# Forgetting attention and a bilinear FFN on one core: q and k turned on VectorE, scores of four heads on row quarters

## The chip, the cores and the metric

The kernel runs on one core of a Trainium2 chip. The core has a matrix engine (TensorE, "PE" in the profile, whose weight loads are listed apart as "PEld"), VectorE ("DVE"), ScalarE ("ACT") and GpSimd ("POOL"), each with its own in-order queue of instructions, and a queue "SP" that issues transfers. All work from SBUF, 128 partitions wide; TensorE writes to PSUM, which has eight banks of 512 float32 columns per partition. The metric is the device time in microseconds.

## The reference

Batch 8, 8 heads, 576 positions, 64 elements per head; FFN with model width 512 and inner width 1536, over 8 x 576 = 4608 tokens.

```python
scores = 0.125 * q @ k.T                      # per batch and head, 576 x 576
cum    = cumsum(log(clip(f, 1e-4, 1)))        # per batch and head
scores = where(causal, -1e9, scores + cum[i] - cum[j])
attn   = softmax(scores, -1);  o = attn @ v
x      = o, heads side by side: (4608, 512)
out    = ((x @ w_a) * (x @ w_b)) @ w_out      # (4608, 512)
```

In the softmax cum[i] is constant along a row and drops out, so the kernel only subtracts cum[j].

## The kernel before, in words

Work is cut into operations (`Op`). A list of numbers written out by hand, `ORDER` (line 1016), gives the sequence in which all operations are issued; each engine takes its own in that order. `CHOICE` (line 1123) is a string of letters that says which engine does an operation that several could do. What waits for what is worked out from the tiles that the operations touch.

There are 32 head pairs t = 0 to 31, four to a batch. A pair here is head pr and head pr + 4 of batch b = t // 4.

- **Inputs** (`batch_inputs`, line 310). q and k come in halves, four loads a batch, nine tokens of each of two heads on a partition; GpSimd casts them to 16 bits (in batch 0 ScalarE and VectorE help). `pe_transpose` (279) turns a half on TensorE: 18 transposes of 64 columns into two PSUM tiles of the ring "ff". `pe_evict` (290) copies each to qT or kT on ScalarE or VectorE, so that a head's 64 elements lie on partitions 0 to 63 or 64 to 127.
- **Scores** (`qk_group`, 411). The causal rows are cut into row blocks i = 0 to 4 (four of 128 queries, one of 64), in stages (1, 0), (2), (3), (4). Two heads are computed at once, on the two row halves of the array. The last block of 64 queries of both heads uses the whole array, with the queries laid out block-diagonally in `qd` by GpSimd (`last_queries`, 474). The score tiles "sc" hold two PSUM banks each, and there are two of them.
- **Decay and mask.** In batch 0 the decay row and the causal mask are added by further matmuls (`crow`, `pick`, `low`, `neg`); in batch 1 the decay row is spread to all partitions by a matmul (`spread_mm`, 480); from batch 2 on it is loaded from DRAM (`load_spread`, 491) and masked on GpSimd (`mask_copy`, `mask_last`).
- **Softmax.** VectorE adds the decay and takes the maximum in one instruction per head and block (`do_decay`, 516, line 540 in the profile; in batch 0 only a maximum, 514), ScalarE takes the exponential (571, 567), VectorE the reciprocal, GpSimd scales the probabilities (`do_norm`, 583, line 589).
- **Turning the probabilities.** In batch 0 on TensorE (`pe_tr`, 605) with evictions; from batch 1 by transposing transfers on SP's queue (`do_tr`, 599).
- **Values** (`do_pv`, 618, and `do_pv4`, 636 for the last 64 queries): for each key block and row block one matmul of 128 columns per head, the two heads on the two column halves. From batch 2 on, a pair's values are computed two pairs later, right after the score stage 0 of that later pair, and the last 64 queries' values go to a spare corner of that stage's score tile.
- **FFN** (`ffn`, 952). Token chunks of 256, 256, 256, 384, six of 512, and 384. Each needs all attention of its tokens. Twelve steps: `psa` and `psb` (four matmuls each, line 914), a copy of psa to SBUF (`ff_copy`), a product on VectorE (`ff_mul`, 925); then `pso` (934), an eviction and a store for each 128 tokens.

PSUM: two "sc" tiles of two banks, one "pv" bank, three "ff" banks. TensorE's order mixes FFN groups of earlier tokens between the attention stages of later ones.

Of the kernel before, what the change touches and what calls it, by code (L numbers as in the profile page):

```python
# [15 lines left out]
ADD = mybir.AluOpType.add  # L16
MIN = mybir.AluOpType.min
MAX = mybir.AluOpType.max

NEGBIG = -60000.0  # L20
SUB = mybir.AluOpType.subtract
AXX = mybir.AxisListType.X
# [3 lines left out]
def kernel(  # L26
# [17 lines left out]
    sbw = [min(128, S - 128 * i) for i in range(NSB)]  # L44
    BH = B * H
    NP = H // 2
    SF = 512
    ST = S - SF

    def pool(name, bufs=1, **kw):  # L50
        return ctx.enter_context(tc.tile_pool(name=name, bufs=bufs, **kw))

    perm = pool("perm")

    HP = [slice(0, 64), slice(64, 128)]
    dram = pool("scr", 1, space=bass.MemoryType.DRAM)

    neg64 = perm.tile([128, 64], FP16, tag="neg64", name="neg64")  # L60
    low = [perm.tile([128, 128], FP16, tag=f"low{i}", name=f"low{i}") for i in range(2)]

    qd = [perm.tile([128, 128], FP16, tag=f"qd{i}", name=f"qd{i}") for i in range(2)]
    lowd = perm.tile([128, 128], FP16, tag="lowd", name="lowd")

    crow = perm.tile([128, S], FP16, tag="crow", name="crow")
    pick = perm.tile([128, 32], FP16, tag="pick", name="pick")
    pickh = [perm.tile([128, 32], FP16, tag=f"pick{h}", name=f"pick{h}") for h in range(2)]
    ident16 = perm.tile([128, 128], FP16, tag="ident16", name="ident16")
    warm = perm.tile([128, 1], FP32, tag="warm", name="warm")  # L70

    def constants():
        make_identity(nc, ident16)
        for x in pickh:
            nc.gpsimd.memset(x, 0.0)
        for m in range(4):
            x = slice(32 * m, 32 * m + 32)
            nc.gpsimd.tensor_copy(out=pick[x, :], in_=ident16[x, x])
            nc.gpsimd.tensor_copy(out=pickh[m // 2][x, :], in_=ident16[x, x])
        nc.gpsimd.memset(neg64, 0.0)  # L80
        for x in low:
            nc.gpsimd.memset(x, 1.0)
        for h in range(2):
            nc.gpsimd.affine_select(out=neg64[HP[h], :], in_=neg64[HP[h], :],
                                    compare_op=mybir.AluOpType.not_equal, fill=NEGBIG, base=0,
# [6 lines left out]
    def paddings():  # L92
        for x in (*qd, lowd):
            nc.gpsimd.memset(x, 0.0)
        for r in HP:
            nc.gpsimd.tensor_copy(out=lowd[r, r], in_=low[0][r, 0:64])
# [104 lines left out]
    for o in o_f:  # L201
        o.issue, o.units = 0.5, 32
# [968 lines left out]
```

## Time and profile before

| | |
|---|---|
| median of 3 runs | 418.18 us (417.76 to 418.24) |
| span of the profiled execution | 416.2 us |
| busy: TensorE, VectorE, ScalarE, GpSimd | 386.7, 298.1, 283.4, 265.7 us |
| first FFN matmul | 35.58 us |
| scores, on TensorE (tile sc, last-query values in it) | 59.4 us busy |
| q/k transposes, on TensorE | 15.65 us busy |
| FFN, on TensorE (psa, psb, pso) | 115.25, 115.33, 98.78 us busy |

The profiled execution's span, 416.2 us, runs from its first to its last instruction; the runs' times also have some 2 us around it. A row of the groups of instructions reads: source line, engine, operation, output <- inputs, for matmuls the shape rows*columns of the array that is used, shapes, count, then busy time and mean duration of one in ns, then the idle time before the group and what ended it. A row of the timeline reads: start, duration, engine, line, operation, count. Matmuls overlap, so the time that one costs is the distance to the next start and not its duration.

### The profile page before, as it was taken

Reading aid. Unit: us, or ns where it says so; the run is one execution under the profiler, and the core shown is the slowest. Engines: PE = TensorE matmul, PEld = TensorE weight load, DVE = VectorE, ACT = ScalarE, POOL = GpSimd, SP = SyncE. Lnnn points to the kernel's source line nnn. Section 1 sums busy time; section 2 is a strip of 40 time slices with the busy share of each in tenths; the row PEclk is TensorE's granted clock in tenths of the full one; section 3 lists DMA queues with packets and bytes.
Section 4 is the critical chain, followed back from the end, with each engine's and each line's share of the span. In section 5 each row is a group of like instructions: output and inputs, shape, how many; then the busy total and the mean of one; then the engine's idle time right before and its main releaser. Section 6 shows DMA issues by size and latency. Waiting matters only on the chain.

```text
span 416.2 us, 10864 instructions
## 1 busy us (share of the span) xinstructions
PE 386.7 (93%) x3788; PEld 207.7 (50%) x3788; DVE 298.1 (72%) x1000; ACT 283.4 (68%) x797; POOL 265.7 (64%) x491
## 2 busy tenths in 40 slices
PE   2678999998989999999999999999999999999996
PEld 1346775756645544444454444454454444444552
DVE  3697998997878878786877888777877785332240
ACT  5788998986766877876777887677767783232231
POOL 5998998786677868875686787857758645000000
PEclk9999999999999999999999999999999999999999
DMA  8899999999999999999889999989988266200201
GB/s 268 176 221 255 231 214 217 202 227 252 233 244 264 264 228 247 245 228 250 212 189 246 273 225 204 252 190 265 231 145 229 57 153 144 80 1 25 78 1 76
DMA packets 153431, 80.56 MB, mean 194 GB/s; under 512 B 130720, under 2 KB 133280, under 8 KB 153376
## 3 DMA queue, kind: packets, MB, share of 16 engines
q1 hardware_dynamic: 149616, 75.15, 78.9%
q0 software_dynamic: 3760, 4.72, 6.7%
q8 instruction: 29, 0.48, 0.5%
q14 instruction: 26, 0.21, 0.2%
HBM read 52.05 MB, written 9.58 MB: 148 GB/s over the span
## 4 chain that ended last, share of the span: by engine, by line
PE 47%; DVE 5%; DMA 1%; issue 1%; ACT 1%; SPq 0%; DVEq 0%; ACTq 0%
PE pso L934 14%; PE psa L914 13%; PE psb L914 13%; DVE S L540 3%; PE sc L417 3%; PE pv L631 2%; DMA v<-in_v_dram 1%; DVE ht L925 1%; PE sc L647 1%; PE psT L285 1%; ACT PA L571 0%; DVE st L540 0%; ACT qT L240 0%; DVE st L581 0%; DVE xT L244 0%
## 5 line engine op out<-in xcount | busy, mean ns | idle before, releaser
L540 DVE CUSTOM_DVE_ANT_0 S<-sc,spread 64x576 f32<-64x576 f32 (+4 forms) x232 | 125.8, 561 | 10.7 <-PE sc L417 5.2
L914 PE MATMUL psb<-xT,wb 128*128 128x512 f16 (+2 forms) x528 | 115.3, 341 | 1.2 <-ACT qT L240 1.0
L914 PE MATMUL psa<-xT,wa 128*128 128x512 f16 (+2 forms) x528 | 115.2, 341 | 0.4
L240 ACT CAST a<-psa 128x512 f16<-128x512 f32 (+2 forms) x132 | 66.3, 503 | 56.4 <-PE psa L914 46.0
L589 POOL TENSOR_SCALAR PA<-PA,st 128x256 f16<-128x256 f16 (+2 forms) x192 | 90.4, 481 | 20.4 <-DVE st L581 11.2
L925 DVE TENSOR_TENSOR ht<-psb,a 128x512 f16<-128x512 f32 (+2 forms) x132 | 77.7, 590 | 33.1 <-PE psb L914 29.4
L934 PE MATMUL pso<-wout,ht 128*128 128x512 f16 x432 | 98.8, 379 | 0.3 <-DVE ht L925 0.2
L571 ACT ACTIVATE PA<-S,st 128x256 f16<-128x256 f32 (+2 forms) x168 | 84.4, 504 | 15.7 <-DVE st L540 14.7
L589 POOL TENSOR_SCALAR PB<-PB,st 128x512 f16<-128x512 f16 (+1 forms) x96 | 67.6, 713 | 23.9 <-DVE st L581 16.2
L914 PEld LDWEIGHTS <-wa 128*128 128x128 f16 x528 | 49.1, 98 | 41.4 <-issue 3.0
L914 PEld LDWEIGHTS <-wb 128*128 128x128 f16 x528 | 48.7, 98 | 40.7 <-issue 2.8
L934 PEld LDWEIGHTS <-ht 128*128 128x128 f16 x432 | 40.5, 98 | 47.2 <-issue 2.0
L571 ACT ACTIVATE PB<-S,st 128x512 f16<-128x512 f32 x56 | 40.2, 718 | 13.1 <-DVE st L540 11.7
L417 PE MATMUL sc<-kT,qT 64*128 64x128 f16 (+4 forms) x384 | 35.7, 271 | 4.6 <-DVE kT L244 2.0
L571 ACT ACTIVATION_READ_ACCUMULATOR PA<-S,st 128x1 f32 x168 | 31.9, 190 | 0.0
L581 DVE RECIPROCAL st<-st 128x2 f32<-128x2 f32 x128 | 19.2, 158 | 14.0 <-ACT PB L571 8.6
L244 DVE CAST xT<-pv 128x512 f16<-128x512 f32 (+1 forms) x40 | 23.0, 576 | 7.4 <-PE pv L631 7.2
L567 ACT ACTIVATE PB<-S,st 128x576 f16<-128x576 f32 x28 | 21.7, 776 | 9.4 <-issue 4.2
L417 PEld LDWEIGHTS <-qT 64*128 64x128 f16 (+1 forms) x384 | 13.6, 95 | 26.3 <-issue 21.0
L240 ACT COPY osb<-pso 128x512 f32<-128x512 f32 x19 | 11.0, 576 | 22.5 <-PE pso L934 16.1
L499 POOL TENSOR_SCALAR_AFFINE_SELECT spread<-spread 128x768 f32<-128x768 f32 x24 | 20.9, 869 | 8.3 <-DMA spread<-cum_d 8.0
L631 PEld LDWEIGHTS <-nv 128*64 128x64 f16 x640 | 19.2, 109 | 12.4 <-issue 9.3
(91 smaller groups left out, 440.0 us busy)
## 6 DMA issues: line engine op xcount, KB each, us to landing
spread<-cum_d SPq DMA_DIRECT2D x24, 576.0 KB, 5.8
out_dram<-osb SPq DMA_DIRECT2D x36, 256.0 KB, 3.1
q<-in_q_dram SPq DMA_DIRECT2D x15, 576.0 KB, 7.0
k<-in_k_dram SPq DMA_DIRECT2D x15, 576.0 KB, 5.1
v<-in_v_dram SPq DMA_DIRECT2D x32, 256.0 KB, 6.1
wout<-in_moe_w_out_dram POOLq DMA_DIRECT2D x3, 512.0 KB, 6.4
v<-in_v_dram SPq DMA_DIRECT2D x8, 128.0 KB, 7.5
wb<-in_moe_w_b_dram POOLq DMA_DIRECT2D x2, 512.0 KB, 9.6
```

The source lines that it names most:

```text
L240: nc.scalar.copy(out=out_, in_=in_)
L244: VEC[e].tensor_copy(out=out_, in_=in_)
L417: nc.tensor.matmul(out=dst, lhsT=lhsT, rhs=rhs, start=start, stop=stop, skip_group_check=True)
L499: nc.gpsimd.affine_select(out=c[:, :, 0:SM].rearrange("p h (j k) -> p h j k", k=128), in_=c[:, :, SM:2 * SM].rearrange("p h (j k) -> p h j ...
L540: nc.vector.tensor_tensor_reduce(out=o, in0=x, in1=y, scale=-1.0, scalar=3e38, op0=ADD, op1=MIN, accum_out=m)
L567: nc.scalar.activation(out=p_blocks(t, 4), in_=T[("s" if direct else "z", t, 4)], func=EXP, bias=st[:, 8:9], scale=sign, accum_out=st[:, 1 ...
L571: nc.scalar.activation(out=p_blocks(t, i)[:, :, h, :], in_=(T[("s", t, i)][:, h, :] if direct else T[("z", t, i)][:, h * n:h * n + n]).rea ...
L589: VEC[e].tensor_scalar(out=p, in0=p, scalar1=st[:, c:c + 1], scalar2=1.0, op0=MUL, op1=MUL)
L631: nc.tensor.matmul(out=o[HP[h], 128 * i:128 * i + 128], lhsT=vt[:, j, pr + NP * h, :], rhs=pt[:, base_blk[i] + 2 * block_at(t, i, j) + h, ...
L914: nc.tensor.matmul(out=p[:, 0:n], lhsT=w16[:, db, 128 * fb:128 * fb + 128], rhs=xTflat[db][:, t0:t0 + n], start=(db == 0), stop=(db == 3))
L925: nc.vector.tensor_tensor(out=ht[:, 0:n], in0=T.pop(("psb", t0, fb))[:, 0:n], in1=T.pop(("a16", t0, fb))[:, 0:n], op=MUL)
L934: nc.tensor.matmul(out=o, lhsT=T[("ht", t0, fb)][:, 128 * tb:128 * tb + 128], rhs=wout16[:, fb, :], start=(fb == 0), stop=(fb == 11))
```

## The change

The kernel is rewritten in many places, with a new ORDER and CHOICE. What it does:

- A pair is now two neighbouring heads, and q and k are loaded four heads at a time: 32 partitions per head, 18 tokens of it on each (`load_qk`). The cast interleaves tokens in twos (`cast_qk`), and one VectorE transpose of 32x32 blocks of four-byte elements (two tokens each) per load writes qT or kT (`transpose_qk`), so that a head lies on 32 partitions with its 64 elements in two halves `dh`. The TensorE transposes and their evictions are gone.
- Scores of two pairs (`u` = 0 to 15) are one stage: four heads on the four row quarters, each in two passes that accumulate. A stage takes both "sc" tiles. The last 64 queries go the same way; `qd` and `last_queries` are gone, and their mask comes from a further GpSimd instruction on the loaded row (`mask_tail`).
- Batch 0 goes block by block over its four pairs (`first_attention`), each pair alone on two quarters. f is loaded eight times over the partitions from ScalarE's queue, and its cumulative sum split into high and low parts on VectorE.
- Value matmuls from batch 2 on stream up to 384 columns. Their evictions may go to ScalarE; the copies of psa may go to VectorE.
- Rings: decay rows 3 to 4, PA 4 to 3, PTA 3 to 2, "ff" 3 to 4 banks with "pv" now in it. Batch 0 keeps two pairs' probabilities in the decay rows' tiles (`HOME`).
- 60 matmuls on the identity run first on TensorE (`warming`). Weights of the FFN come in 7 loads instead of 11.

```diff
+    RING = {"S": 2, "bc": 4, "n32": 3, "n16": 2, "PA": 3, "PB": 2, "PTA": 2, "PTB": 2, "st": 6, "ht": 14, "a16": 3, "osb": 2, "ff": 4}
...
+    def warming(_):
+        p = ps.tile([128, 512], FP32, tag="ff", bufs=RING["ff"], name="idle")
+        for n in range(60):
+            nc.tensor.matmul(out=p[:, 0:128], lhsT=ident, rhs=ident, start=True, stop=True)
...
+    def rows_part(lo, hi):
+        nc.vector.scalar_tensor_tensor(out=crow[:, lo:hi], in0=chigh[:, lo:hi], scalar=lsel,
+                                       in1=cw["f"][0][:, lo:hi], op0=MUL, op1=ADD)
...
+    def load_qk(b, which, hh):
...
+        src = src_of[which][b, 4 * hh:4 * hh + 4].rearrange("h (s t) d -> (h s) (t d)", s=NSLOT)
+        nc.sync.dma_start(out=x, in_=src)
+
+    def cast_qk(e, b, which, hh, lo, hi):
...
+            T[key] = n16_pool.tile([128, TW, D, 2], FP16, tag="n16", name=f"{which}16")
+        x = T[("n32", which, b, hh)].rearrange("p (w e d) -> p w d e", w=TW, e=2)
+        cast(e, T[key][:, lo:hi], x[:, lo:hi], which == "q")
...
-    def pe_transpose(b, which, half):
-
-        x = T[("n16", which, b, half)].rearrange("p t h d -> p t (h d)")
-        p = [ps.tile([128, 1024], FP16, tag="ff", bufs=3, name="psT") for _ in range(2)]
-        for t in range(TG):
-            for m, r in enumerate(HP):
-                nc.tensor.matmul(out=p[m][:, 64 * t:64 * t + 64], lhsT=x[r, t, :], rhs=ident16[r, r], is_transpose=True,
-                                 start=(t == 0), stop=(t == TG - 1), skip_group_check=True)
...
-    def pe_evict(e, b, which, pr):
...
+    def transpose_qk(b, which, hh):
+        if ("T", which, b) not in T:
+            T[("T", which, b)] = qkT_pool.tile([128, 2, 2, S], FP16, tag=f"{which}T", name=f"{which}T")
+        x = T[("n16", which, b, hh)].rearrange("p w d e -> p (w d e)").bitcast(FP32)
+        y = T[("T", which, b)][:, hh].rearrange("p a s -> p (a s)").bitcast(FP32)
+        nc.vector.transpose(out=y.rearrange("p (a s w) -> p w a s", a=2, s=NSLOT),
+                            in_=x.rearrange("p (w a d) -> p w a d", a=2, d=32))
...
+    def qk_group(u, g, ws=(0, 1)):
+        b, hh = divmod(u, 2)
...
+        c = {w: ps.tile([128, 2, 512], FP32, tag="sc", bufs=2, name=f"sc{g}") for w in ws}
+        heads = [(c[w], h, RG[2 * w + h], 8 * b + 4 * hh + 2 * w + h) for w in ws for h in range(2)]
...
+        if g == 3:
+            for x, lo, hi in ((0, 0, SF), (1, SF, S)):
+                for dh in range(2):
+                    for y, h, r, _ in heads:
+                        mm(y[HP[h], x, 0:hi - lo], qT[r, hh, dh, SF:S], kT[r, hh, dh, lo:hi], start=dh == 0, stop=dh == 1)
...
+            for j0, j1 in key_runs(t0, i):
+                n = 128 * (j1 - j0)
+                for dh in range(2):
+                    for y, h, r, _ in heads:
+                        mm(y[:, h, col:col + n], qT[r, hh, dh, 128 * i:128 * i + 128], kT[r, hh, dh, 128 * j0:128 * j1],
+                           start=n_ == 0, stop=dh == 1)
...
-    def last_queries(t):
...
+    def mask_tail(t):
+        x = spread[t % RING["bc"]][:, :, SM + SF:SM + S]
+        nc.gpsimd.affine_select(out=x, in_=x, compare_op=GE, fill=NEGBIG, base=0,
+                                pattern=[[-64, 2], [-1, 64]], channel_multiplier=1)
...
+        if b >= EARLY:
+            a, c = T[("PT", "A", t)], T[("PT", "B", t)]
+            at = {0: (0, 4), 1: (2, 8), 2: (6, 1)}
+            for j in range(4):
+                for h in range(2):
+                    lhsT = vt[:, j, 2 * pr + h, :]
+                    if j < 3:
+                        n0, step = at[j]
+                        x = a[:, n0 + h:n0 + h + step * (2 - j) + 1:step, :]
+                        nc.tensor.matmul(out=o[HP[h], 128 * j:384], lhsT=lhsT, rhs=x, start=j == 0, stop=j == 2,
+                                         skip_group_check=True)
+                    nc.tensor.matmul(out=o[HP[h], 384:512], lhsT=lhsT, rhs=c[:, 2 * j + h, :], start=False, stop=j == 3,
+                                     skip_group_check=True)
+            return
...
+        turn = (0, 1, 2, 3) if early else (0, 1, 3, 2)
+        for g in turn:
...
+            qk = op("E", f"qk{g}" + ("e" if early else ""), lambda _, g=g: qk_group(u, g), deps)
...
+            sc_of[g] = [take(qk, "sc") for _ in range(2)]
...
+    def first_attention():
...
+        for g in range(4):
+            for t in range(NP):
+                u, w = divmod(t, 2)
...
+                qk = op("E", f"qk{g}d", lambda _, g=g, u=u, w=w: qk_group(u, g, (w,)), deps)
```

More of the change, by code (lines that the diff above doesn't have):

```diff
@@ L114, with fixed @@
[L114 to L116 removed]
+    def fixed(name, shape, dt=FP16):
+        return perm.tile(shape, dt, tag=name, name=name)
+    ident = fixed("ident", [128, 128])
+    eye = fixed("eye", [128, 32])
+    neg = fixed("neg", [128, 32])
+    step = fixed("step", [128, 32])
+    pick = fixed("pick", [128, 16])
```

1130 lines of the change are left out of this document (490 added, 640 removed), and 155 rows, old and new, of the table ORDER.

## The prediction

> **What bounds the kernel now.** I read the page first, then busy time by stage, with cuts at the first FFN matmul (35.58 us), at 100 and 356 us, and at the last matmul.
>
> ```profile
> span 416.2 us, 10864 instructions
> PE 386.7 (93%) x3788; PEld 207.7 (50%) x3788; DVE 298.1 (72%) x1000; ACT 283.4 (68%) x797; POOL 265.7 (64%) x491
> PE   2678999998989999999999999999999999999996
> ...
> 0.00:35.58 35.58, 19.45 (x301) 11.89 (x301) 23.43 (x54) 26.44 (x76) 30.38 (x76) 1.00 0.97 227
> 35.58:100.00 64.42, 63.00 (x850) 43.49 (x845) 57.91 (x215) 56.00 (x170) 53.16 (x89) 1.00 1.14 228
> 100.00:356.00 256.00, 247.95 (x2346) 124.68 (x2343) 198.10 (x703) 185.83 (x525) 182.16 (x327) 1.00 0.95 216
> 356.00:412.24 56.24, 56.24 (x307) 27.62 (x302) 18.71 (x31) 14.56 (x27) 0.00 (x0) 1.00 0.10 38
> ```
>
> In the stage rows the columns after the length are busy PE, PEld, DVE, ACT and POOL. From 35.58 us on TensorE idles 1.42 + 8.05 + 0 = 9.5 us: the order of its work is the bound there, so each microsecond of matmul time or drain taken out of this stretch counts. Before 35.58 us it idles 16.1 us, and the vector engines set the pace. Busy hides drains, so stage costs are taken from distances between starts in TensorE's timeline:
>
> ```profile
> 204.47 1.03 PE L914 MATMUL psa<-xT,wa 128*128 128x512 f16 x4
> 205.44 0.34 PE L417 MATMUL sc<-kT,qT 64*128 64x128 f16 x4
> 205.71 1.04 PE L914 MATMUL psb<-xT,wb 128*128 128x512 f16 x4
> 206.58 1.03 PE L914 MATMUL psa<-xT,wa 128*128 128x512 f16 x4
> ...
> 208.40 0.36 PE L631 MATMUL pv<-PTA,nv 128*64 128x128 f16 x6
> ...
> 208.98 0.32 PE L647 MATMUL sc<-PTB,nv 128*64 128x64 f16 x10
> 209.24 1.04 PE L914 MATMUL psa<-xT,wa 128*128 128x512 f16 x4
> ...
> 216.81 0.43 PE L285 MATMUL psT<-ident,q 64*128 64x64 f16 x18
> 217.07 0.33 PE L417 MATMUL sc<-kT,qT 64*128 64x128 f16 x4
> ...
> 221.95 0.41 PE L417 MATMUL sc<-kT,qd 128*128 128x512 f16 x2
> ...
> 222.22 1.89 PE L934 MATMUL pso<-wout,ht 128*128 128x512 f16 x8
> 224.04 0.39 PE L417 MATMUL sc<-kT,qT 64*128 64x512 f16 x2
> 224.37 3.63 PE L934 MATMUL pso<-wout,ht 128*128 128x512 f16 x16
> ```
>
> Four FFN matmuls of 512 columns start 0.86 us apart, 0.216 us each. After 204.47 the next FFN group could start at 205.33; the row-half scores start at 205.44 and the FFN resumes at 205.71: 0.11 us of drain on entry, 0.16 us of work (384 columns, two heads at once, 0.42 ns a column), 0.11 us on exit. The full-array detour at 221.95 costs 0.27 us and no drain.
>
> **The change on TensorE, part by part.**
>
> (a) Stage work of batches 2 to 7, per head pair. Before: scores 0.16 + 0.16 + 0.21 (512 columns, 224.04 to 224.37 less drains) + 0.27 = 0.80 us; values 0.58 us (208.40 to 208.98, twenty matmuls) and 0.15 for the last 64 queries (208.98 to 209.24 less the drain); one transpose stage 0.26 us (216.81 to 217.07). Sum 1.79. After: the scores of two pairs go together, four heads on four row quarters, each in two passes of 32 rows. With all four overlapped that is 768 + 768 + 1024 + 1152 = 3712 columns by 0.42 ns, 1.55 us for two pairs, 0.77 for one. The bound is two at a time, as 205.44 shows it for halves: 1.55 for one. I take full overlap: the psT row has 18 matmuls with a weight load each in 0.26 us, 15 ns apiece, so four loads take about 0.06 us against 0.053 us of streaming at 128 columns, and issue does not stand in the way. Values: the first three key blocks now stream 384, 256 and 128 columns, 14 matmuls instead of 20; at 0.42 ns the seven pairs need 1280 columns, 0.53 us, plus 0.15. Sum 1.45, so 0.34 less for each of 24 pairs: **-8.2 us**.
>
> (b) Drains. Counted in the timeline from 36 to 372 us, the array shape changes 198 times, first and last here:
>
> ```profile
> 37.35 0.60 PE L914 MATMUL psb<-xT,wb 128*128 128x256 f16 x4
> 37.88 0.25 PE L631 MATMUL pv<-xT,nv 128*64 128x128 f16 x2
> ...
> 360.04 0.35 PE L647 MATMUL pv<-PTB,nv 128*64 128x64 f16 x10
> 360.32 1.04 PE L914 MATMUL psb<-xT,wb 128*128 128x512 f16 x4
> ```
>
> In the new ORDER, from its first FFN group to its end, the same count is 153, since one score stage serves two pairs, though the last-query scores now leave the full array (32 by 64). 45 fewer at 0.10 us: **-4.5 us**. Two transpose stages of batch 1 also lie behind 35.58 us: **-0.5 us**.
>
> (c) Work of batch 0 left over when the FFN starts:
>
> ```profile
> 35.58 0.61 PE L914 MATMUL psa<-xT,wa 128*128 128x256 f16 x4
> ...
> 36.46 0.61 PE L609 MATMUL psP<-ident,PB 128*128 128x128 f16 x8
> 36.91 0.60 PE L914 MATMUL psa<-xT,wa 128*128 128x256 f16 x4
> ...
> 39.11 0.39 PE L417 MATMUL sc<-kT,qT 64*128 64x512 f16 x2
> ...
> 40.35 0.61 PE L914 MATMUL psa<-xT,wa 128*128 128x256 f16 x4
> ```
>
> Two score stages like the one at 39.11 (1.24 us each) and 70 of 100 probability blocks (0.056 us each, 36.46 to 36.91) still follow here. The new order has all scores and 52 blocks before its first FFN group: -2.4 - 1.2 = **-3.6 us**.
>
> (d) The first FFN group. Batch 0 runs per pair on two quarters, so its score passes double: 4 x 0.8 = 3.2 us more, twice that while the array is slow, in the 16.1 us of idle; without that cover 3 to 6 us. The 60 warming matmuls also lie there, before any data. The path is VectorE's. Now:
>
> ```profile
> 9.90 0.89 DVE L187 TENSOR_TENSOR_SCAN cum_f<-cum_f,cum_l 96x320 f32<-96x320 f16 x1
> 13.67 0.48 ACT L571 ACTIVATE PA<-sc,st 128x256 f16<-128x256 f32 x1
> 17.41 0.58 PE L482 MATMUL scd<-crow,pick 128*128 128x512 f16 x1 [2.95 <-POOL crow L192]
> ...
> L514 DVE TENSOR_REDUCE st<-sc 128x2 f32<-128x1024 f32 x4 | 4.9, 1219 | 0.3 <-PE sc L417 0.3
> ```
>
> f now loads from ACT's queue ahead of everything and GpSimd's row splitting (2.95 us of wait at 17.41) is gone, so exponentials start near 11 us instead of 13.67. But ahead of the last value eviction that the FFN needs, VectorE has some 13 us of maxima (1.22 us for the 512-key row block, the others in proportion), 3.5 of transposes and 6.5 of evictions and reciprocals: dense from about 11, 34 us. Bounds 32 to 40; I take 35.0: **-0.6 us**.
>
> (e) Other engines:
>
> ```profile
> L244 DVE COPY kT<-psT 128x576 f16<-128x576 f16 x8 | 6.0, 753 | 0.8 <-PE psT L285 0.7
> L240 ACT COPY qT<-psT 128x576 f16<-128x576 f16 x26 | 15.9, 640 | 3.1 <-PE psT L285 3.1
> L240 ACT COPY kT<-psT 128x576 f16<-128x576 f16 x24 | 14.5, 636 | 1.3 <-PE psT L285 1.2
> L244 DVE CAST xT<-pv 128x512 f16<-128x512 f32 x24 | 16.4, 683 | 6.2 <-PE pv L631 6.1
> L244 POOL CAST k<-k 128x1152 f16<-128x1152 f32 x14 | 16.0, 1144 | 2.4 <-PE sc L417 2.4
> L478 POOL COPY qd<-qT 64x64 f16<-64x64 f16 x48 | 11.2, 233 | 1.4
> L506 POOL TENSOR_SCALAR_AFFINE_SELECT spread<-spread 128x256 f32<-128x256 f32 x24 | 9.8, 408 | 21.6 <-DVE st L540 21.5
> ```
>
> 64 evictions go (50 of ACT, 30.4 us, and 14 of VectorE, at 753 ns 10.5); 32 VectorE transposes come, 576 four-byte elements written 36 bytes apart. Nearest row: 753 ns for 576 elements read with a stride; bounds 0.6 (a shade under it) and 1.5 us (double). I take 0.75: +24 us. [...] The choices also put 40 of 132 a-copies on VectorE (0.6 us each, from the 683 ns row by columns: +24 us) and 19 of 24 value evictions on ACT (19 x 0.683 = -13). Between 100 and 356 us VectorE rises from 198 to about 208 us, of some 244: 85%. GpSimd loses the qd copies (-11), gains 24 tail masks of half the 408 ns row's size (0.27 each with its fixed part, +6.5), and its 28 q/k casts now read pairs 256 bytes apart: 1.14 us each as now, bound 1.7 (half more, +16 in all). ACT falls by some 25. SP issues the same loads, stores and probability transposes, ordered by pairs; each pair's transposes wait for GpSimd and, with PTA two deep, for the values two pairs back; next q, k, v loads queue behind them. None of these reaches TensorE's total, so all count as hidden, but VectorE has less slack: idle 9.5 becomes 12.5, **+3 us** (bounds 0 and +24).
>
> Sum: -8.2 - 4.5 - 0.5 - 3.6 - 0.6 + 3 = -14.4, span 401.8. The profiled execution's span is 416.2 and the median 418.18, 2.0 us around it: **403.8 us**.
>
> **Rivals.**
> *Score tiles run dry in pairs* (slower). "sc" stays two tiles deep, and one stage now takes both: the next cannot start until both pairs' VectorE reads are done, where now one tile fills while the other is read. For it: four stages in each of 14 double pairs, VectorE at 85%. Against: the order puts two to four FFN groups (1.7 to 3.4 us) between stages. At 0.4 us of stall per stage, 56 stages lose 22 us in place of the 3: 423 us. It decides above (14.4 + 3)/56 = 0.31 us a stage.
> *Quarters overlap only in pairs* (slower). 14 x 1.55 = 21.7 us: 425 us. Against it, halves overlap fully at 205.44.
> *Quarters overlap in part.* At three quarters of the full rate 14 x 0.5 = 7 us: 411 us. [...] No run here shows quarters yet.
> *Strided transposes and casts are dear.* VectorE +24 (32 x 0.75 more), GpSimd +16: VectorE at about 93% of the stage. Were a third of the 24 to reach TensorE, 412 us.
>
> **How the numbers follow.** Forecast 0.55 (396 to 410: start 3 us either way, idle 0 to 9); dear transposes 0.10 and partial overlap 0.08, both still faster; dry score tiles 0.17, pairs only 0.08; no change 0.02. Faster 0.73, same 0.02, slower 0.25; 0.2% (0.8 us) is about what a measurement tells from no change. Leaving out the slowest cases and the best start gives 394 to 423.
>
> **What would show it.** Right: no psT rows; score stages x16 or more with starts 0.32 to 0.48 us apart, drains aside; first FFN matmul near 35 us; TensorE idle after it near 12 us; transposes near 0.75 us. Wrong: waits of TensorE's scores on VectorE's decay line worth over 15 us; scores above 2 us per double pair; VectorE over 92% between 100 and 340 us.

## The result and the profile after

The changed kernel takes 421.96 us (median of 20 runs, 418.47 to 426.86) against 419.37 us for the kernel before (20 runs): ratio 1.0069, 95% interval 1.0042 to 1.0096. It is 0.7% slower, where 403.8 us was forecast. Times here and below are medians of all runs of a kernel, while ratios leave out runs more than 1.5% above that kernel's shortest. The profiled execution took 424.4 us, 2.4 above the median.

Its page (span, TensorE's total, and in 40 slices TensorE's busy share and granted clock), then busy time by stage with cuts at the first FFN matmul, at 100 and 356 us and at the last matmul (columns: length, PE, PEld, DVE, ACT, POOL, clock, DMA share, GB/s):

```profile
span 422.6 us, 10576 instructions
PE 393.6 (93%) x3712; PEld 210.9 (50%) x3712; DVE 323.4 (77%) x1020; ACT 255.5 (60%) x760; POOL 257.1 (61%) x436
PE   5379999988999998999999999999899999999996
PEclk9555599999999999999999999999999999999999
...
0.00:52.13 52.13, 36.72 (x410) 25.11 (x411) 36.05 (x77) 32.96 (x92) 33.18 (x60) 0.59 1.02 230
52.13:100.00 47.87, 44.55 (x682) 32.06 (x681) 44.96 (x178) 40.68 (x135) 39.73 (x69) 0.98 1.01 221
100.00:356.00 256.00, 249.69 (x2270) 122.86 (x2270) 217.50 (x724) 170.46 (x514) 183.90 (x309) 1.00 0.91 213
356.00:418.66 62.66, 62.66 (x354) 30.86 (x351) 24.85 (x41) 10.85 (x20) 0.32 (x1) 1.00 0.17 54
```

The first FFN matmul starts at 52.13 us instead of 35.58: 16.55 us lost. From it to the end of the span pass 422.6 - 52.13 = 370.5 us instead of 416.2 - 35.58 = 380.6: 10.1 us gained (13.8 were forecast). Together +6.4. So the change did most of what it should in the long stretch, and lost more than that in batch 0, where the granted clock shows a row of 5s: in this execution the array ran at half speed, a granted clock of 0.50, from about 10 to 53 us.

The rows of TensorE's timeline that answer to the forecast of the score stages, and one stage of batch 0 ahead of the first FFN matmul (start, duration):

```profile
42.49 1.17 PE L389 MATMUL sc<-kT,qT 32*64 32x512 f16 x8
43.48 0.66 PE L389 MATMUL sc<-xT,pick 32*64 32x512 f16 x4
...
52.13 1.06 PE L866 MATMUL psa<-xT,wa 128*128 128x256 f16 x4
...
240.74 0.52 PE L389 MATMUL sc<-kT,qT 32*128 32x128 f16 x24
241.19 1.04 PE L866 MATMUL psa<-xT,wa 128*128 128x512 f16 x4
...
252.49 0.69 PE L389 MATMUL sc<-kT,qT 32*64 32x512 f16 x16
253.10 0.36 PE L599 MATMUL pv<-PTA,nv 128*64 128x384 f16 x2
...
257.34 0.61 PE L389 MATMUL sc<-kT,qT 32*128 32x512 f16 x8
257.88 1.04 PE L866 MATMUL psb<-xT,wb 128*128 128x512 f16 x4
```

With four heads on four quarters, 768 columns take 0.45 us, 1152 take 0.61 and 1024 take 0.54, each with about 0.11 us of drain (the 0.11 us that 204.47 to 205.71 showed before the change): 0.42 to 0.44 ns a column. These are undisturbed stages. In others the second pair starts late, as the weight loads of a stage of 1152 columns show:

```profile
118.03 0.10 PEld L389 LDWEIGHTS <-qT 32*64 32x64 f16 x2 [0.21 <-DVE st L504]
118.40 0.14 PEld L389 LDWEIGHTS <-qT 32*64 32x64 f16 x8 [0.26 <-DVE st L504]
...
118.03 1.05 PE L389 MATMUL sc<-kT,qT 32*64 32x512 f16 x16
119.01 0.36 PE L599 MATMUL pv<-PTA,nv 128*64 128x384 f16 x2
```

Here the stage takes 0.98 us instead of 0.61: the first pair's two heads start at 118.03 and the second pair's at 118.40, after VectorE's decay instruction (L504) has read their score tile.

At 42.49 us, in batch 0, two heads on two quarters, 1152 columns each, take 0.99 us without a drain, at a granted clock of 0.50: 0.86 ns a column.

The groups of instructions that take the place of TensorE's transposes and their evictions (line, engine, operation, shapes, count, then busy us and mean ns):

```profile
L300 DVE STREAM_TRANSPOSE qT<-q 128x576 f32<-128x576 f32 x16 | 19.4, 1210 | 0.7 <-POOL q L139 0.6
L300 DVE STREAM_TRANSPOSE kT<-k 128x576 f32<-128x576 f32 x16 | 19.3, 1208 | 1.4 <-POOL k L141 1.4
L139 POOL TENSOR_SCALAR q<-q 128x1152 f16<-128x1152 f32 x14 | 19.7, 1404 | 4.5 <-DVE qT L300 2.6 <-DMA q<-in_q_dram 1.9
L141 POOL CAST k<-k 128x1152 f16<-128x1152 f32 x14 | 19.5, 1396 | 2.4 <-DMA k<-in_k_dram 2.4
L463 POOL TENSOR_SCALAR_AFFINE_SELECT spread<-spread 128x128 f32<-128x128 f32 x24 | 7.1, 295 | 1.3 <-DMA spread<-cum_d 1.3
```

And batch 0 itself: VectorE's largest groups between 9 us and the first FFN matmul, its wait for f, and ScalarE's first exponential:

```profile
L481 DVE TENSOR_REDUCE st<-sc 128x2 f32<-128x512 f32 (+4 forms) x20 | 15.8, 802 | 5.9 <-PE sc L389 5.8
L300 DVE STREAM_TRANSPOSE kT<-k 128x576 f32<-128x576 f32 x4 | 4.8, 1195 | 0.0
L300 DVE STREAM_TRANSPOSE qT<-q 128x576 f32<-128x576 f32 x3 | 3.6, 1188 | 0.0
L141 DVE COPY xT<-psP 128x768 f16<-128x768 f16 x5 | 2.7, 547 | 0.9 <-PE psP L579 0.9
L547 DVE RECIPROCAL st<-st 128x2 f32<-128x2 f32 x16 | 2.2, 151 | 0.2 <-ACT PB L537 0.2
...
DVE cum_f L208 <- DMA cum_f<-in_f_dram: 5.5, 1, 5.5
...
17.50 0.47 ACT L537 ACTIVATE PA<-sc,st 128x256 f16<-128x256 f32 x1 [0.70 <-DVE st L481]
```

The first exponential comes at 17.50 us; before it came at 13.67, and the forecast had 11.

### The profile page after: what moved, and what is told of

Read it like the earlier page. It is cut to its first block, busy times and chain, and to the rows that moved or that the text cites. A ratio compares the mean times of both kernels' runs of the same rounds, so it can differ in the third digit from the quotient of the medians.

```text
span 422.6 us, 10576 instructions
## 1 busy us (share of the span) xinstructions
PE 393.6 (93%) x3712; PEld 210.9 (50%) x3712; DVE 323.4 (77%) x1020; ACT 255.5 (60%) x760; POOL 257.1 (61%) x436
## 5 line engine op out<-in xcount | busy, mean ns | idle before, releaser
L504 DVE CUSTOM_DVE_ANT_0 S<-sc,spread 128x384 f32<-128x384 f32 (+4 forms) x232 | 124.0, 562 | 15.5 <-PE sc L624 5.6
L555 POOL TENSOR_SCALAR PA<-PA,st 128x128 f16<-128x128 f16 (+2 forms) x180 | 83.4, 478 | 40.5 <-DVE st L547 26.6
L877 DVE TENSOR_TENSOR ht<-psb,a 128x512 f16<-128x512 f32 (+2 forms) x132 | 76.2, 587 | 22.1 <-PE psb L866 17.4
L137 ACT CAST a<-psa 128x512 f16<-128x512 f32 (+2 forms) x92 | 45.4, 498 | 50.9 <-PE psa L866 46.9
L389 PE MATMUL sc<-kT,qT 32*128 32x128 f16 (+5 forms) x960 | 55.4, 284 | 20.5 <-DVE qT L300 8.0
L866 PEld LDWEIGHTS <-wb 128*128 128x128 f16 x528 | 49.8, 98 | 45.6 <-issue 6.1
L555 POOL TENSOR_SCALAR PB<-PB,st 128x512 f16<-128x512 f16 (+1 forms) x90 | 62.7, 710 | 15.2 <-DVE st L547 9.6
L389 PEld LDWEIGHTS <-qT 32*128 32x128 f16 (+1 forms) x960 | 23.5, 99 | 48.2 <-issue 24.8
L141 DVE CAST a<-psa 128x512 f16<-128x512 f32 (+2 forms) x40 | 23.6, 592 | 3.5 <-PE psa L866 3.1
L504 DVE DVE_READ_ACCUMULATOR2_ANT st<- 128x1 f32 (+1 forms) x280 | 22.9, 82 | 0.0
```

The costliest lines, as they stand in the source:

```text
L137: nc.scalar.copy(out=out_, in_=in_)
L141: ENG[e].tensor_copy(out=out_, in_=in_)
L389: nc.tensor.matmul(out=dst, lhsT=lhsT, rhs=rhs, start=start, stop=stop, skip_group_check=True)
L504: nc.vector.tensor_tensor_reduce(out=o, in0=x, in1=y, scale=-1.0, scalar=3e38, op0=ADD, op1=MIN, accum_out=m)
L555: ENG[e].tensor_scalar(out=p, in0=p, scalar1=st[:, c:c + 1], scalar2=1.0, op0=MUL, op1=MUL)
L866: nc.tensor.matmul(out=p[:, 0:n], lhsT=w16[:, db, 128 * fb:128 * fb + 128], rhs=xTflat[db][:, t0:t0 + n], start=(db == 0), stop=(db == 3))
```

## The experiments

Two theories at first. *Slow array*: batch 0 on two row quarters never brings the clock up, and TensorE at half speed holds up the first FFN group. *The rest of batch 0*: f, the loads, or VectorE's work set its pace, and the clock is an onlooker.

**What raises the clock, and what a transpose costs (m1_clock).** A kernel of its own with eight stretches of matmuls, and between them VectorE operations of 576 four-byte elements.

> A kernel of its own, computing nothing of the reference: eight stretches of TensorE work, some 20 us each, with a gap of twelve VectorE operations (576 four-byte elements) before each. In order: whole array, two halves, two quarters, four quarters, one quarter, transposes, whole array and then two quarters, one half; all 512 columns but the transposes. Theory 'two quarters stay slow': whole array, two halves and four quarters start at 0.43 us per step (a step is one matmul on each row group) and fall to 0.216 after some microseconds; two quarters stay at 0.43 throughout, and after the whole array has made the clock fast, two quarters lose it again within some microseconds. Rival 'gaps alone': every kind gets fast after the same time, two quarters too, since it is only the gaps between stages that kept the array slow. For VectorE: transposes written straight 0.75 us and written 36 bytes apart 1.2 us (the stride is the cost), or both 1.2 us (the operation is); copies written 36 bytes apart show the stride's cost without a transpose.

It took 255.71 us. Busy time of TensorE in each stretch with its mean granted clock (length, PE with its count, clock): whole array, two halves, two quarters, four quarters, one quarter, 128-column transposes, two quarters after a whole-array start, one half:

```profile
14.29:26.48 12.19, 12.18 (x44) 1.00 0.00 0
42.07:54.04 11.97, 11.96 (x88) 0.80 0.00 1
69.32:95.10 25.78, 25.78 (x120) 0.50 0.00 1
101.82:112.93 11.11, 11.11 (x176) 0.87 0.01 2
123.48:142.41 18.93, 18.93 (x44) 0.50 0.00 1
158.00:171.61 13.61, 13.61 (x200) 0.82 0.01 1
193.90:215.73 21.83, 21.82 (x201) 1.00 0.00 1
231.30:250.23 18.93, 18.93 (x44) 0.50 0.00 0
```

Two quarters without a gap for 25.8 us leave the clock at 0.50, and so do one quarter and one half for 18.9 us. Four quarters raise it some 3.0 us after their start, two halves 4.7, whole-array work (182.15) 4.6 and the 128-column transposes 4.8, worked out from the mean clock of the 4 us in which it changes: 0.90, 0.66, 0.66 and 0.65. (The 1.00 of the first stretch is no reading, see below: it has 12 matmuls between 16 and 20 us and 20 between 20 and 24.) Once up, two quarters without a gap hold it (193.90, 201 matmuls in 21.83 us at 1.00), where the expectation had them lose it.

VectorE's four kinds in the same kernel (all source elements adjacent; the second and third write 36 bytes apart):

```profile
L59 DVE STREAM_TRANSPOSE d<-d 128x576 f32<-128x576 f32 x36 | 28.0, 779 | 1.2
L62 DVE STREAM_TRANSPOSE d<-d 128x576 f32<-128x576 f32 x36 | 43.2, 1200 | 1.2
L66 DVE COPY d<-d 128x576 f32<-128x576 f32 x12 | 14.1, 1175 | 0.4
L70 DVE COPY d<-d 128x576 f32<-128x576 f32 x12 | 5.5, 460 | 0.4
```

The stride, not the turning, makes the kernel's transposes cost 1.2 us: written side by side they take 0.78, and a copy 36 bytes apart takes 1.18 without any turning.

**Warming (x1_nowarm, x3_warm260).** The 60 matmuls at the start become 1, or 260.

```diff
-        for n in range(60):
+        for n in range(1):      # x3_warm260: range(260)
```

> The changed kernel with 1 warming matmul instead of 60. Theory 'two quarters stay slow': the warm clock is lost in the 8 us before the first scores anyway, so the time stays within 1 us of the changed kernel, first FFN matmul at 52 us. Rival 'the warming itself leaves the array slow': the array gets fast near 25 us as in the kernel before, first FFN matmul 5 us or more earlier.

> The changed kernel with 260 warming matmuls, which keep the array busy until about the first scores at 15 us. If two quarters keep a clock that is already fast, batch 0 runs at 0.42 ns a column and the first FFN matmul comes 8 us or more earlier. If two quarters lose it, as the theory has it, the array is slow again within about 5 us of the first scores and the first FFN matmul stays within 2 us of 52.

One matmul: 424.12 us, ratio 1.0168 (1.0122 to 1.0215), first FFN matmul at 52.57 us, so the 60 bring nothing here that can be told from the spread between chips (the changed kernel itself had 1.015 on another, see a0_after). 260: 421.78, ratio 1.0107 (1.0072 to 1.0142), first FFN matmul at 48.27. There the clock fell at about 22 us (0.70 between 20 and 24, 0.50 after) and rose again at about 39 (0.67 between 36 and 40), well before that matmul: both answers that were set down beforehand, 8 us or more and less than 2, missed. The start gained 3.9 us on the profile after; the span gained 1.1.

The run with one matmul also shows how not to read the clock. Its slices say full speed, and its rows say half, 0.98 us for the stage that took 0.99 above:

```profile
PEclk9999999969999999999999999999999999999999
...
42.93 1.17 PE L389 MATMUL sc<-kT,qT 32*64 32x512 f16 x8
43.91 0.66 PE L389 MATMUL sc<-xT,pick 32*64 32x512 f16 x4
```

In these records the clock stands at 1.00 ahead of its first change, whatever the distances say. The kernel before shows the same thing: 9s throughout, but a pass of 384 columns takes 0.30 us at 17.92 and 0.27 at 21.20, against 0.16 from 23.29 on:

```profile
17.92 0.50 PE L417 MATMUL sc<-kT,qT 64*128 64x384 f16 x2
18.22 0.53 PE L417 MATMUL sc<-crow,pick 64*128 64x384 f16 x2
...
21.20 0.51 PE L417 MATMUL sc<-kT,qT 64*128 64x384 f16 x2 [0.30 <-ACT PA L571]
21.47 0.55 PE L417 MATMUL sc<-crow,pick 64*128 64x384 f16 x2
...
23.29 0.34 PE L417 MATMUL sc<-kT,qT 64*128 64x384 f16 x2 [0.25 <-ACT PA L571]
23.45 0.34 PE L417 MATMUL sc<-crow,pick 64*128 64x384 f16 x2
```

**The early weight loads (x2_wlate).** 2 MB of FFN weights are issued at 1.5 to 5.3 us now, at 18 us before, a move that the prediction did not count. Here they go back behind the first scores.

```diff
+        for n, behind in ((46, 241), (47, 46), (48, 51)):
+            seq.remove(ops[n])
+            seq.insert(seq.index(ops[behind]) + 1, ops[n])
```

> The changed kernel with the first three FFN weight loads (2 MB read) behind the q cast of batch 1 and the second w_out load on GpSimd's queue, near 21 and 28 us instead of 1.4 to 5 us. Theory 'early transfers crowd out f, q and k': f lands near 5 us instead of 9, the first exponential moves from 17.5 to about 13.5 us, and the first FFN matmul comes 4 us earlier, the time falls by 3 to 4 us. Rival 'the slow array alone sets the start': first exponential earlier, first FFN matmul within 1 us of 52.

431.73 us, ratio 1.0327 (1.0277 to 1.0377). The first exponential came at 17.30 instead of 17.50, so f is not held up by the weights; the late weights met the loads of v, for which ScalarE waited 9.5 us, and the first FFN matmul slid to 58.08. The early loads are not the cause.

**Clock and stride, each alone and together (a0_after, j1_clock, s1_straight, js_both).** One chip for all four; a0_after is the changed kernel again.

> The changed kernel itself, to stand beside the three below on the same chip. Theory 'slow array' and theory 'VectorE backlog' alike: ratio 1.007 to the kernel before, first FFN matmul at about 52 us.

423.93 us, ratio 1.015 (1.0095 to 1.0205), first FFN matmul at 51.62.

```diff
+        if b < DIRECT and g < 2:                       # j1_clock, with 220 warming matmuls
+            for x in range(12):                        # after the scores, into unread columns of their tile
+                mm(c[ws[0]][:, x % 2, 384:512], ident, ident)
```

> 220 instead of 60 warming matmuls, and 12 (8 for the last rows) full-array matmuls of 128 columns behind each score stage of batch 0, into columns that nobody reads. Theory 'slow array' (batch 0 on two row quarters never raises the clock, and TensorE at half clock holds up the first FFN group): clock at full from about 7 us on, distance of two 384-column passes 0.16 instead of 0.32 us, first FFN matmul at 42 to 46 us instead of 52, and the kernel 5 to 9 us shorter than the unchanged one. Rival 'VectorE backlog' (VectorE is dense up to 100 us, so what TensorE gains there it waits for later, as with 260 warming matmuls): first FFN matmul earlier all the same, but the kernel at most 2 us shorter. If the doubled passes hurt by something else than the clock: first FFN matmul stays above 50 us.

423.96 us, ratio 1.0102 (1.0043 to 1.0161). A failed experiment: the maxima came behind the filling, which lies in the same tile, so that the first exponential came at 18.28 us, and the clock fell at 22.3 us all the same; first FFN matmul at 53.81.

```diff
-        nc.vector.transpose(out=y.rearrange("p (a s w) -> p w a s", a=2, s=NSLOT),
-                            in_=x.rearrange("p (w a d) -> p w a d", a=2, d=32))
+        nc.vector.transpose(out=y, in_=x)              # s1_straight
```

> The 32 transposes of q and k write their output contiguously instead of 36 bytes apart; the tokens of q and k come out in another order, which leaves out the sorting and nothing else. Both theories: 0.78 instead of 1.20 us a transpose, 13.4 us less VectorE work, 20 of the 32 before 100 us. Theory 'slow array': first FFN matmul stays at 51 to 52 us, where TensorE is busy without a gap, and the kernel is at most 2 us shorter. Rival 'VectorE backlog': 4 to 8 us shorter, most of it between 52 and 100 us.

418.77 us, ratio 0.999 (0.9957 to 1.0023): 5.2 us shorter than a0_after. The first FFN matmul came at 47.55. The gain is larger than the slow-array theory allowed for this edit, and 4.1 us of it lie ahead of the first FFN matmul, where the VectorE theory had most of it behind. But it is not free of the clock:

```profile
30.00:40.00 10.00, 7.43 (x94) 4.81 (x96) 8.17 (x16) 6.70 (x19) 8.98 (x18) 0.61 1.12 225
40.00:50.00 10.00, 8.90 (x181) 6.82 (x177) 9.27 (x24) 9.71 (x23) 9.13 (x13) 1.00 1.13 210
```

In this execution the clock rose at about 38 us; in a0_after it stood at 0.50 until after 50 us.

> Both edits. Theory 'slow array' alone: as the clock edit by itself, within 2 us. Both causes together: first FFN matmul at 38 to 43 us, and the kernel 9 to 14 us shorter than the unchanged one, more than the sum of the two edits alone.

422.87 us, ratio 1.0081 (1.0048 to 1.0115), first FFN matmul at 54.14: the failed filling hides what the transposes bring.

**A filling that holds the clock (k1_fill).** In a tile of its own, ahead of the scores:

```diff
+        if b < DIRECT:                                 # with 220 warming matmuls
+            p = ps.tile([128, 512], FP32, tag="ff", bufs=RING["ff"], name="idle")
+            for x in range((24, 24, 12)[g]):
+                mm(p[:, 0:128], ident, ident, start=True, stop=True)
```

> 220 warming matmuls, and ahead of each score stage of batch 0 (12 of the 16) 24 full-array matmuls of 128 columns, 12 for the 512-key rows, into a tile of their own, where TensorE waits for a score tile anyway. Theory 'slow array': clock at full from 7 us to the end, starts of two 384-column passes 0.16 us apart, first FFN matmul at 43 to 48 us, kernel 4 to 8 us shorter than the unchanged one (ratio to the kernel before 0.995 to 1.005). Rival 'VectorE and the score tiles set the pace of batch 0 whatever the clock': first FFN matmul at 50 us or later, kernel within 2 us of the unchanged one.

421.24 us, ratio 1.0068 (1.004 to 1.0096), first FFN matmul at 49.85. The clock is held, but TensorE is now dense with filling:

```profile
10.00:20.00 10.00, 10.00 (x194) 9.62 (x191) 8.22 (x14) 7.46 (x15) 3.13 (x3) 1.00 1.13 293
20.00:30.00 10.00, 10.00 (x190) 8.61 (x185) 8.71 (x18) 7.49 (x34) 6.16 (x11) 1.00 1.06 233
```

That it is held is read from the 194 matmuls in 10 us, some 50 ns each, where 128 columns at 0.86 ns would take 110. The outcome is nearer to the rival's (50 us or later, within 2 us of the changed kernel) than to the slow array's (43 to 48): the ratio equals the 1.0069 of the first series and is 0.008 below a0_after's. So this run alone doesn't show that the clock matters. It is a lower bound for what the clock is worth, since it pays with 220 + 240 matmuls.

**Writing without the stride, order kept (c1_short).** Neighbouring token pairs on neighbouring partitions, which needs 512-byte pieces and four issues a load.

```diff
+        for h in range(4):
+            src = src_of[which][b, 4 * hh + h].rearrange("(w s e) d -> s w (e d)", s=NSLOT, e=2)
+            nc.sync.dma_start(out=x[RG[h]].rearrange("p (w c) -> p w c", w=TW), in_=src)
```

> q and k loaded so that neighbouring token pairs stand on neighbouring partitions (pieces of 512 instead of 4608 bytes, four issues a load), and the transposes written in runs of 128 bytes. Full computation. If the 36-byte stride is what costs, 0.78 to 0.85 us a transpose and a kernel 4 to 6 us shorter, as with contiguous writes. Rival 'short pieces cost in the DMA engines': loads of q and k land 2 us or more later, first exponential 1 to 3 us later, and the kernel no shorter than the unchanged one.

448.51 us, ratio 1.0683 (1.0608 to 1.0759). The transposes fell to 0.77 us, and the loads paid for it: SP's queue (start, us) with the same load of q in both kernels, first here, then in the changed kernel:

```profile
7.55 9.70 SPq L287 DMA_DIRECT2D wout<-in_q_dram  x4
```

```profile
1.66 0.56 SPq L286 DMA_DIRECT2D wout<-in_q_dram  x1
```

The four issues took 9.7 us, the first exponential came at 26.54, and TensorE idled 11 us between 100 and 200.

**FFN groups earlier (r1_ffn), and both (b1).** Four steps of the first FFN chunk between the last score stages.

```diff
+    key[232] = 181.5
+    for fb in range(4):
+        for x in range(4):
+            key[1635 + 4 * fb + x] = 182 + 2.5 * fb + 0.1 * x
```

> The first four pairs of FFN matmul groups moved in the written order from behind to between the last score stages of batch 0. Theory 'slow array': full-array work at about 46 us brings the clock up at 48 to 50 instead of 53.6 us, and the kernel is 2 to 5 us shorter than the unchanged one. Rival 'VectorE backlog': first FFN matmul earlier, kernel within 1 us of the unchanged one.

> The loads in short pieces and the earlier FFN groups together. If both gains are real and add, 6 to 10 us shorter than the unchanged changed kernel: 413 to 418 us, at or below the kernel before. If the loads in short pieces cost what they bring, as the earlier FFN groups alone.

r1_ffn: 428.16 us, ratio 1.014 (1.0075 to 1.0204). The first FFN matmul came at 45.35, and the time went elsewhere:

```profile
50.00:60.00 10.00, 8.33 (x155) 6.28 (x155) 8.68 (x28) 8.55 (x20) 6.93 (x10) 1.00 0.23 67
60.00:70.00 10.00, 8.19 (x106) 5.41 (x106) 7.96 (x31) 8.99 (x31) 9.44 (x16) 0.66 1.02 180
```

These rows are of a run of 431.06 us; the two shorter runs, 423.74 and 425.25, are no shorter than the changed kernel either. TensorE, full from 40 us to the first FFN matmul in the changed kernel and nearly full after, now idles 3.5 us, and the clock falls once more. An earlier first FFN matmul is not worth anything by itself: what it is put in front of comes later. b1: 453.63 us, 1.0837 (1.079 to 1.0883), first exponential at 26.25; the loads in short pieces decide it, as in c1_short.

**VectorE's maxima left out (v1_nomax).**

```diff
-        nc.vector.tensor_reduce(out=m, in_=T[("s", t, i)], axis=AXX, op=MAX, negate=True)
+        nc.vector.memset(m, 0.0)          # and the exponentials of batch 0 with scale 0
```

> The 20 maxima of batch 0 are left out (a constant in their place, and the exponentials of batch 0 run with scale 0, so they take the same time). Theory 'VectorE's own work before the first FFN group sets its time': 15 us of VectorE work less, first FFN matmul at 38 to 43 us, kernel 7 to 12 us shorter than the unchanged changed kernel. Rival 'slow array': TensorE still needs 33 us at half clock, first FFN matmul at 47 us or later, kernel 2 to 5 us shorter. Rival 'ScalarE's exponentials': ScalarE has 31 us of work from 9 us on, first FFN matmul at 41 us or later.

423.38 us, median of 10 runs (416.27 to 425.4), ratio 1.004 (0.9988 to 1.0093). The profiled execution, the shortest of all, had its first FFN matmul at 45.27, the earliest of all profiles, and the clock up at about 37 us. Seven of the ten runs have a granted clock of 0.943 to 0.950, as the profile after has, and a mean of 423.7 us; the changed kernel's own seven runs at that clock have 424.8, on a chip where the kernel before was 1.5 us longer too. Taking 15 us off VectorE in batch 0 gained next to nothing there: while the array stays at half speed to the end of batch 0, VectorE is not what batch 0 waits for.

**Both causes away (sk), and a lighter filling (k2, sk2).** sk is s1_straight with k1_fill. k2 has 190 warming and 14, 14, 8 filling matmuls, sk2 also contiguous transposes.

> Contiguous transposes (order of the tokens left out) and the filled array together. If both causes are real and add, 5 + 2 us shorter than the unchanged changed kernel: ratio to the kernel before 0.990 to 0.997, first FFN matmul at 44 to 47 us. If they are the same gain (the contiguous transposes help only because the clock rises earlier): ratio 0.997 to 1.003, as with contiguous transposes alone.

> 190 warming matmuls and 14 (8 for the 512-key rows) filling matmuls a stage. Full computation. If the clock's price is larger than the first filling showed, and 14 a stage hold it: clock at full throughout, first exponential at 17.5 to 18.5 us, first FFN matmul at 44 to 47 us, kernel 416 to 419 us, as fast as the kernel before or faster. If 2 to 3 us is all that the clock is worth: first FFN matmul at 49 us or later and 420 to 422 us. If the filling does not hold the clock: it falls between 20 and 40 us, and nothing is gained.

> The same with contiguous transposes (order of the tokens left out). If the two gains are separate: 4 to 6 us shorter than k2, 411 to 415 us, ratio to the kernel before 0.983 to 0.993. If the contiguous transposes gained by the clock alone: within 2 us of k2.

sk: 417.49 us, ratio 0.9999 (0.9967 to 1.003), first FFN matmul at 50.27. That is the outcome set down for "the same gain": no shorter than contiguous transposes alone (0.999). k2: 425.54, sk2: 419.11 (12 and 13 runs; ratios 1.0055, 1.0005 to 1.0104, and 0.999, 0.9956 to 1.0025). The lighter filling holds the clock in some executions and loses it in others, and the program is the same in both. Means in us by the granted clock of the run:

```
kernel   clock held (over 0.98)    clock lost (0.967 to 0.976)
k2       420.27, 4 runs            425.88, 8 runs
sk2      417.12, 7 runs            424.12, 6 runs
         granted clock 0.958 up    below
after    420.86, 10 runs           423.94, 10 runs
s1       417.30, 6 runs            420.66, 4 runs
```

Runs that lose the clock are 5.6 and 7.0 us longer. A small part of that is the filling itself: 24 of its matmuls lie in the stretch that is slow in k2's profile. The changed kernel's own runs and those of s1_straight, which have no filling, differ by 3.1 and 3.4 us. These are sortings of runs and not edits: an execution that is late for another reason would lose the clock too. The profiles of k2 and sk2 fell on executions that lost it: k2's clock went at about 31 us and its first FFN matmul came at 55.24; no trace of one that held it was kept. Contiguous transposes gain 3.2 us with the clock held and 1.8 with it lost (k2 to sk2, one chip), 3.6 and 3.3 in the two halves without filling (after to s1_straight, two chips whose kernel before differs by 0.8). They gain whether the clock is held or not, so the transposes are a cause of their own. The expectation that sk2 would be 411 to 415 us failed all the same: 417.1.

**Half the stride (t1c, t1k).** Three pieces of 1536 bytes, written 12 bytes apart; t1k with k1's filling.

```diff
+        src = src_of[which][b, 4 * hh:4 * hh + 4].rearrange("h (w s x) d -> w h s (x d)", w=3, s=NSLOT)
+        for w in range(3):
+            nc.sync.dma_start(out=x[:, 384 * w:384 * w + 384], in_=src[w])
```

> q and k loaded in three pieces of 1536 bytes a partition instead of one of 4608, and the transposes written 12 instead of 36 bytes apart. Full computation. If the price of the stride falls with the stride, 0.8 to 0.95 us a transpose and a kernel 3 to 5 us shorter than the unchanged one. If every stride costs alike, 1.2 us and no gain. Rival 'pieces cost in the DMA engines': first exponential 2 us or more later, and 2 us or more longer.

> The same with the filled array: 2 to 3 us shorter than without the filling; if both gains hold, 413 to 418 us and shorter than the kernel before.

538.79 and 536.83 us, ratios 1.2877 (1.2814 to 1.2939) and 1.2852 (1.2815 to 1.2889). The transposes went to 0.95 us, between the 0.78 and 1.20 of m1_clock, but the loads crawled (last columns: clock, DMA share, GB/s):

```profile
L301 DVE STREAM_TRANSPOSE kT<-k 128x576 f32<-128x576 f32 x16 | 15.2, 952 | 33.3 <-POOL k L141 26.7 <-ACT k L137 6.6
...
20.00:30.00 10.00, 0.00 (x0) 0.00 (x0) 0.46 (x1) 2.10 (x3) 0.00 (x0) 0.50 0.27 84
```

The sixteen DMA engines stood at a mean share of 0.27, 84 GB/s, while everything waited for q, and the three issues of that load took 11.06 us on SP's queue (from 13.76), where the one issue of the changed kernel takes 0.56. Short pieces alone are not it: with pieces of 512 bytes the share between 20 and 30 us was 1.24, at 198 GB/s (c1_short). What else in the description of the load makes it slow, no run took apart.

No version with the whole computation beats the kernel before. The nearest is k2 in the executions that keep the clock, 417.5 to 422.4 us, against a median of 417.54 before in the same series.

## Why the prediction was wrong

The step that failed is (d), the start that was to be covered by idle time. A smaller miss lies in (e), the waits of score stages for their tiles.

(a) *Stage work of batches 2 to 7.* Right for undisturbed stages. Four quarters run at the full rate (0.45 us at 240.74), the values take 0.55 us where 0.53 were reckoned, and the rivals "quarters only in pairs" and "in part" are out.

(b) *Drains.* Right: 151 changes of the array's shape after the first FFN group, 153 forecast, 198 before.

(e) *Other engines.* The transposes came to 1.21 us, inside the bounds of 0.6 and 1.5 but far above the 0.75 taken; the casts to 1.40 where 1.14 was taken and 1.7 the bound. The nearest row had misled: 753 ns was a copy out of PSUM in 16 bits, where here four-byte elements are written 36 bytes apart, and in m1_clock that stride alone takes a copy from 0.46 to 1.18 us. VectorE was busy 217.5 us between 100 and 356, where 208 were forecast; the prediction's own terms add up to some 24 more over the whole kernel, and 25 were measured. TensorE's idle time after the first FFN group is nevertheless only 3.3 + 6.3 = 9.6 us, not 12.5.

From the first FFN matmul on, 10.1 us were gained where 13.8 were forecast. Since the idle time was overestimated by 2.9, some 6.5 us are missing in TensorE's busy time. Most of them are the rival "score tiles run dry", at half its price. In the trace after, 26 of the 48 score stages of batches 2 to 7 start their second pair late, by 0.09 to 1.56 us, as at 118.03. Each time the weights of the second pair load within 0.1 us after an instruction that reads a score tile has ended, nearly always VectorE's. That makes 10.2 us, 0.21 a stage, where the prediction set the line at 0.31. Only some 4 of them are in the 9.6 us of idle time; in the other 6 the array holds a first pair that runs alone, and the profile calls it busy.

(d) *The first FFN group* came at 52.13 us, forecast 35.0, bounds 32 to 40. It had two terms.

TensorE's term was called hidden: doubled score passes of 3.2 us, "twice that while the array is slow", in 16.1 us of idle. The mistake is in *while*. Two quarters alone did not raise the clock in m1_clock (0.50 through 25.8 us), and in the profiled execution all of batch 0 from 10 us on stayed slow (0.50 until after 52 us), the transposes of its probabilities and its values with it. In x3_warm260, s1_straight and v1_nomax the clock came back at 37 to 39 us, 8 to 10 us ahead of the first FFN matmul, so batch 0 has enough other work to raise it at times. TensorE had 36.7 busy us of the first 52 and no gap between 40 and 52. There the cover was gone, for which the prediction itself had given 3 to 6 us. Measured, in k2 and sk2, runs that lose the clock for some 20 us are 5.6 to 7.0 us longer. (Some 20, because the mean clocks of the two groups differ by about 0.024 over 420 us, and a microsecond at half speed takes half of itself off the mean.)

VectorE's term was put at 23 us from 11 us on. In the profile after, the groups above and the smaller ones beside them sum to about 37 us from 9 us on, some of it overlapping: maxima 15.8 instead of 13, transposes 8.4 instead of 3.5, evictions and reciprocals 7.4 instead of 6.5, and 5.4 us of f's own clipping, sums and splitting that the forecast had left out by starting behind them. And it began later: f lands at 9.07 us, and k and q are turned behind its sums, 1.2 us each.

Which term holds the first FFN group? Both nearly do. With the clock lost, taking the maxima away gains about 1 us at most (v1_nomax). With the clock held and contiguous transposes the kernel stops at 417.1 us (sk2), which would put the first FFN matmul at 45 to 47 us, an estimate: 417.1 less 2 us around the span, less the 370.5 us (after) or 368.3 us (sk) from there to its end. The 10 to 12 us that are still missing to 35 fit the mis-sized VectorE term of 14 us, but no run took that and the clock away together, so this part stays argued, not shown. ScalarE is a rival that no run lightened: between 17.5 and 52.13 us TensorE's scores wait 5.5 us in all for its exponentials. Transfers are hardly one there, since no wait for a load is longer than 1.5 us.

(c) *Leftovers of batch 0* was right in the letter, since all scores of batch 0 now lie ahead of the FFN. But the work of those 3.6 us was not saved: it moved ahead of the first FFN matmul, to the half-speed side, and adds to (d).

The forecast's 0.73 for faster rested on a start that was taken as a number (35.0) and not as a chain with its own bound.

## What to carry over

When an edit narrows the matmuls of a start-up stage, ask first whether the remaining rows still bring the clock up (two quarters stayed at 0.50 for 25.8 us in m1_clock), and price the whole stage at half speed if not, every other matmul in it included. A stage that is "covered by idle time" must be summed engine by engine from its own rows, from the landing of its first input on, before any of it is called hidden. A saving in the long stretch of a kernel is worth what is left after the start it asks for.

## What the runs showed of the hardware

- In m1_clock half of the array's rows, busy without a gap for 25.8 us (two quarters) or 18.9 us (one half), did not raise the granted clock above 0.50; all rows raised it to 1.00 within 3.0 to 4.8 us; two quarters, again without a gap, held 1.00 for 21.8 us once it was up. In j1_clock, by the granted clock in slices of 1 us, it fell at 22.3, rose at 35.9, fell at 39.3 and rose at 42.7 us: distances of 13.6, 3.4 and 3.4 us.
- The recorded clock was 1.00 until its first change, even at half speed: through the whole span in the kernel before, where passes of 384 columns took 0.30 us at 17.92 and 0.16 at 23.29, and at 42.93 us in x1_nowarm, where 1152 columns a head took 0.98 us. Distances between matmuls told the two speeds apart.
- A VectorE operation that writes 576 four-byte elements 36 bytes apart took 1.18 us as a copy and 1.20 us as a transpose (m1_clock); written side by side 0.46 and 0.78 us; turned and written 12 bytes apart 0.95 (t1c).
- With q and k loaded in three pieces of 1536 bytes a partition, the DMA engines stood at a mean share of 0.27 and moved 84 GB/s between 20 and 30 us (t1c); in the changed kernel it was 1.00 and 220 between the same times.
